# The gradient of the convolution kernel: its last quarters computed two steps apart, its stores and two groups of weight-gradient stores issued by ScalarE

## Chip, core and metric

The kernel runs on one core of one Trainium2 chip. The metric is the device time of one execution in microseconds (us). The times given for the kernel before are three runs: 480.13, 480.28 and 480.67 us, median 480.28 us.

## What is computed

The reference takes a normalised input, adds a gated convolution branch and a gated linear branch to it, and returns the output together with the gradients of all nine inputs for a given `grad_out`:

```python
x = A_q; xn = layernorm(x)
kv = causal_shift_conv(k, shift_k) * v              # 4 taps
y  = irfft(rfft(kv, 2S) * rfft(ssm_k, 2S))[:S] + kv * ssm_D
A  = xn * y
B  = ((xn @ w_gate) * (xn @ w_up)) @ w_down
out = x + A + B                                      # out_0
out_1 .. out_9 = vjp(grad_out)                       # q, k, v, shift_k, ssm_k, ssm_D, w_gate, w_up, w_down
```

S is 2048 tokens, D 512 channels, F 1376 hidden features, all arrays are bf16. Four outputs matter here: out_5, the gradient of ssm_k (512 x 2048, 2 MB); out_7 and out_8, the gradients of w_gate and w_up (512 x 1376 each); out_9, the gradient of w_down (1376 x 512).

## The kernel before, in words

The program is written in a tile framework: Python generators emit the instructions of all engines, and the framework puts each engine's instructions in an order, adds the semaphore waits and rotates the buffers. Loads and stores are issued by SyncE (SP, in program order), a few by ScalarE (ACT). All stores of the same engine stand in one queue: a store whose data isn't ready holds back those behind it.

The work comes in three phases. The first and second (up to some 330 us) run the gated linear branch chunk by chunk and, beside it, the transforms of the convolution. The third, `dw()` (L1048), is where the change lies. It goes over the hidden features in eleven blocks `FBLK` (ten of 128 columns, the last of 96), called fb 0 to 10. For each block TensorE computes

- `pd` (`down_grad`, L1022; matmuls in L1036, for the last block in L1029): the block of the gradient of w_down. ACT casts it to `od`, SP stores it to out_9 (L1043). The last block is done in two halves after everything else (L1024 to L1033); its first half is stored by SP, its second by ACT (L1032).
- `pu` (L1060 to L1067): the block of the gradients of w_gate and w_up, as four groups of 16 matmuls with 256 columns (192 for the last block). ACT casts it to `og` (L1073), which holds two blocks; after every second block, and after the last, `og` is stored to out_7 and out_8 (L1074 to L1077). So the stores come after fb 1, 3, 5, 7, 9 and 10. Before the change only those of fb 10 are issued by ACT.
- transposes of the hidden activations for the next block: `pt` (L859), and `pt7` (L829), whose cast `nat7` gives the last two of the 16 token rows.

`dw()` yields six times for each block. At each yield, numbered n, the loop at the end (L1201 to L1206) lets four side generators emit a piece of their own work. Each side is a list `[start, step, generator]`: when n has reached `start`, `step` is added to `start` and one piece is emitted.

```python
sides = [every(seq(inv_y(), load_dk()), 0, 3), every(dsk_gram(), 27, 2), every(inv_dk(), 35, 3), every(ew(), 10, 3)]
```

The third of them, `sides[2]`, is `inv_dk()` (L989): the gradient of ssm_k. It works in quarters `rq` of the 16 token rows, and in halves `b` of the four channel blocks. For each it emits 16 matmuls of 128 columns into a PSUM tile `po` (L1001) and a cast by ACT into `o5t` (L1003), a tile of 128 x 4 x 128 x 16 that is filled quarter by quarter. When a half b of the last quarter (rq 3) is cast, two channel blocks are whole, and each is stored as 512 KB in rows of 4 KB (L1008): four stores in all. In the kernel before, the pieces rq 2 b 1, rq 3 b 0 and rq 3 b 1 fall on n = 53, 56 and 59: after the `pu` of fb 8, ahead of the `pu` of fb 9, and behind it.

The fourth side, `ew()` (L1184), emits the elementwise end on VectorE (DVE): `final` (L1131) and `bwd` (L1108), whose results `o0`, `e` and `dk` are stored by SP (`put_late`, L1179, L1181) to out_0, out_1 and out_2.

PSUM tiles of the kinds `po`, `pu`, `pt7` take turns in three buffers, `pd` in two. DMAs take eight completion semaphores in turn, whichever engine issues them; the built program lets a DMA wait until the last DMA of its semaphore has landed.

Of the kernel before, what the change touches and what calls it, by code (L numbers as in the profile page):

```python
# [24 lines left out]
NFB = len(FBLK)  # L25
# [165 lines left out]
def kernel(  # L191
# [24 lines left out]
    nc = tc.nc  # L216
# [14 lines left out]
    def cs(c):  # L231
        return slice(c * 128, (c + 1) * 128)

    def act(o, i):
        nc.scalar.copy(o, i)  # L235
# [16 lines left out]
    def P2(name, shape, dt=F32):  # L252
        return ps2.tile(shape, dt, name=name, tag="p2")
# [374 lines left out]
    def seq(*its):  # L628
        for it in its:
            for _ in it:  # L630
                yield
# [156 lines left out]
    LG = {}  # L788

    def load_hb(fb):  # L790
        f0, fw = FBLK[fb]
        t = CP["b"].tile([P, NCH - 1, 3, 256], BF, name="hb")
        nc.sync.dma_start(t[:fw], HDD[:fw, fb])
        hbs[fb] = t
# [29 lines left out]
    def last_t(fb):  # L824
        f0, fw = FBLK[fb]
        pt = P2("pt7", [P, 3, 2, P], BF)
        for t in range(3):
            for h in range(2):
                nc.tensor.transpose(pt[:, t, h, :fw], hds[1][:fw, fb, t, h * 128:h * 128 + 128], ident[:fw, :fw])  # L829
        n7 = c2b.tile([P, 3, 2, P], BF, name="nat7", tag="dd")  # L830
        act(n7[:, :, :, :fw], pt[:, :, :, :fw])
        nats[fb, 1] = n7
# [7 lines left out]
    def nat_d(fb, r):  # L840
        f0, fw = FBLK[fb]
        if fb not in TURNED:
            return nats[fb, 1][:, :, r, :fw]
        return nats[fb, 0][r // 2][:, 1:3, r % 2, :] if r < R - 2 else nats[fb, 1][:, 1:3, r % 2, :fw]

    def hid_t(fb, t):
        if fb in TURNED:
            return
        f0, fw = FBLK[fb]
        hb = hbs.pop(fb) if t == 2 else hbs[fb]  # L850
        if t == 0:
            nats[fb, 0] = CP["n"].tile([P, R, P], BF, name="nath")
        elif t == 1:
            nats[fb, 1] = CP["n"].tile([P, 2, R, P], BF, name="natd", bufs=2)
        dst = nats[fb, 0] if t == 0 else nats[fb, 1][:, t - 1]
        pt = P2("pt", [P, R, P], BF)
        for r in range(R):
            hs = hb[:fw, r // 2, t] if r < R - 2 else hds[1][:fw, fb, t]
            nc.tensor.transpose(pt[:, r, :fw], hs[:, (r % 2) * 128:(r % 2) * 128 + 128], ident[:fw, :fw])  # L859
        act(dst[:, :, :fw], pt[:, :, :fw])  # L860
# [114 lines left out]
    def load_gk(rq):  # L975
        return load_g1(2, 4 * rq)
# [3 lines left out]
    def load_gk_last():  # L980
        ts = {}
        for h in range(2):
            for c in range(2):
                t = c2b.tile([P, 2, D], BF, name=("vb", "kb")[c])
                LG["gk"] = nc.sync.dma_start(t[:], GD[2, :, c, 12 + 2 * h:14 + 2 * h, :])
                ts[c, h] = t
        return lambda c, i: ts[c, i // 2][:, i % 2]

    def inv_dk():  # L989
        o5t = c2.tile([P, NC4, P, R], BF, name="o5t", tag="o5k")  # L990
        o5 = out_5.rearrange("(c q) s -> c q s", q=P)
        for rq in range(4):
            gk = gks.pop(0)
            if rq == 0:
                gk_last = load_gk_last()
            for b in range(2):
                po = P2("po", [P, 2, 4, P])
                for h in range(2):
                    for i in range(4):
                        for c in range(2):  # L1000
                            nc.tensor.matmul(po[:, h, i, :], lhsT=(gk_last(c, i) if rq == 3 else gk[:, c, i])[:, cs(2 * b + h)], rhs=TB.IW[:, c, :],  # L1001
                                             start=(c == 0), stop=(c == 1))
                act(o5t[:, 2 * b:2 * b + 2, :, 4 * rq:4 * rq + 4], po[:].rearrange("q h r s -> q h s r"))  # L1003
                if b == 1 and rq < 2:
                    gks.append(load_gk(2) if rq == 0 else None)
                if rq == 3:
                    for c in (2 * b, 2 * b + 1):
                        nc.sync.dma_start(o5[c], o5t[:, c].rearrange("q s r -> q (s r)"))  # L1008
                yield
            if rq == 0:  # L1010
                yield from put_dD(o5t)

    def put_dD(o5t):
        act(dDs[:], o5t[:, :, 0, 0])
        yield
        pt = P1("ptd", [P, P], BF)
        nc.tensor.transpose(pt[:NC4, :], dDs[:], ident[:])
        dDt = c2.tile([NC4, P], BF, name="dDt")
        act(dDt[:], pt[:NC4, :])
        nc.sync.dma_start(out_6.rearrange("(c p) -> c p", p=128), dDt[:])  # L1020

    def down_grad(fb):  # L1022
        f0, fw = FBLK[fb]
        if fb + 1 == NFB:  # L1024
            for h, q in ((0, nc.sync), (1, nc.scalar)):
                hc = slice(256 * h, 256 * h + 256)
                pd = P1("pd", [P, 256])
                for r in range(R):
                    nc.tensor.matmul(pd[:fw, :], lhsT=nat_h(fb, r), rhs=goC[:, r, hc], start=(r == 0), stop=(r == R - 1))  # L1029
                od = c2b.tile([P, D], BF, name="od")  # L1030
                act(od[:fw, :256], pd[:fw])
                q.dma_start(out_9[f0:f0 + fw, hc], od[:fw, :256])  # L1032
            return  # L1033
        pd = P1("pd", [P, D])
        for r in range(R):
            nc.tensor.matmul(pd[:fw, :], lhsT=nat_h(fb, r), rhs=goC[:, r, :], start=(r == 0), stop=(r == R - 1))  # L1036
            if r == R // 2 - 1 and fb:
                hid_t(fb, 2)
                if fb + 2 < NFB:
                    load_h(fb + 2)  # L1040
        od = c2b.tile([P, D], BF, name="od")
        act(od[:fw], pd[:fw])
        nc.sync.dma_start(out_9[f0:f0 + fw, :], od[:fw])  # L1043
# [4 lines left out]
    def dw():  # L1048
        og = None
        load_hb(2)  # L1050
        for fb, (f0, fw) in enumerate(FBLK):
            last = fb + 1 == NFB
            if not last:
                down_grad(fb)
                yield
                hid_t(fb + 1, 0)
                hid_t(fb + 1, 1)
                yield
                yield
            pu = P2("pu", [P, NC4, 2, P])  # L1060
            if fb % 2 == 0:
                og = c2b.tile([P, 2, NC4, P], BF, name="og1", tag="dd") if last else c2.tile([P, 2, NC4, 2 * P], BF, name="og")
            q0 = (fb % 2) * P
            for c in range(NC4):
                for r in range(R):
                    nc.tensor.matmul(pu[:, c, :, :fw], lhsT=xnC[:, r, cs(c)], rhs=nat_d(fb, r),  # L1066
                                     start=(r == 0), stop=(r == R - 1))  # L1067
                if c == 1:
                    yield
                    if fb + 1 in TURNED:  # L1070
                        last_t(fb + 1)
                    yield
            act(og[:, :, :, q0:q0 + fw].rearrange("p t c f -> p c t f"), pu[:, :, :, :fw])  # L1073
            if fb % 2 == 1 or last:  # L1074
                a = f0 - q0
                for t, o in enumerate((out_7, out_8)):
                    LG["og"] = (nc.scalar if last else nc.sync).dma_start(o[:, a:f0 + fw].rearrange("(c p) f -> p c f", p=128), og[:, t, :, :q0 + fw])  # L1077
            yield
            if last:
                down_grad(fb)  # L1080
                yield
# [87 lines left out]
    def every(gen, start, step):  # L1169
        return [start, step, gen]  # L1170
# [13 lines left out]
    def ew():  # L1184
        with tc.issue_after(DKS[2].ins):
            load_fin(0)
        yield
        for f in tail:
            put_late()
            f()  # L1190
            yield
        with tc.issue_after(LG["og"].ins):
            put_late()
        yield

    def load_dk():
        gks.append(load_gk(0))
        gks.append(load_gk(1))
        yield

    sides = [every(seq(inv_y(), load_dk()), 0, 3), every(dsk_gram(), 27, 2), every(inv_dk(), 35, 3), every(ew(), 10, 3)]  # L1201
    for n, _ in enumerate(dw()):
        for sd in sides:
            if n >= sd[0]:
                sd[0] += sd[1]
                next(sd[2], None)  # L1206
# [33 lines left out]
```

## Time and profile before

The profile is of one execution on this core. Its own time was 478.65 us and its span 476.9 us, so 1.75 us lie outside the span; the median of the three timed runs is 480.28 us.

| what | value |
|---|---|
| time of the profiled execution | 478.65 us |
| its span | 476.9 us |
| busy: TensorE (PE), weight loads, DVE, ACT | 98%, 65%, 71%, 64% of the span |
| granted TensorE clock | 0.999 |
| DMA | 139.86 MB, 293 GB/s over the span |
| SP's DMA queue (q1), ACT's (q10) | 137.65 MB, 1.56 MB |
| stores of `o5t` | 4 of 512 KB, 5.2 us from issue to landing (median) |
| stores of `og` | 10 of 256 KB by SP, 6.3 us; 2 of 96 KB by ACT, 4.4 us |

A row of the timeline gives the start, the length, the engine, the line of the code and the tiles (`out<-in`). A name ending in q (SPq, ACTq) is an engine's sequencer: for a DMA the length is that of its issue, and the transfer comes after. A row of the table by stage gives busy time of each engine in a stretch, the TensorE clock, the share of time in which the DMA engines were busy (it can come out a little over 1) and what they moved.

### The profile page before, as it was taken

What the parts mean: (1) busy time and instruction counts of PE and PEld (TensorE: products, weight loads), DVE (VectorE), ACT (ScalarE), POOL (GpSimd) and SP (SyncE); (2) the same over time, 40 slices, a digit from 0 to 9 for tenths busy, and PEclk for the clock granted to TensorE, in tenths of its full rate; (3) what the DMA queues carried; (4) which work ended last, traced back from release to release, by engine and by line L of the source; (5) the groups of instructions that cost most, each with busy time, mean ns of one, the idle gap of its engine ahead of it and who ended that gap; (6) DMA issues with size and microseconds to landing.
All of it is one profiled execution on the core that took longest, in us unless ns stands there. A gap on an engine that the chain in (4) does not pass through costs nothing.

```text
span 476.9 us, 10353 instructions
## 1 busy us (share of the span) xinstructions
PE 465.1 (98%) x4263; PEld 310.7 (65%) x4263; DVE 339.3 (71%) x609; ACT 304.6 (64%) x357; POOL 13.9 (3%) x30
## 2 busy tenths in 40 slices
PE   7999999999999999999999999999999999999995
PEld 6876755547648547447447743567776787777794
DVE  7889979989356567686857877122237899899692
ACT  4957767759577778779879976275675554333331
POOL 8000000000000000000000000110000000000000
PEclk9999999999999999999999999999999999999999
DMA  8999999899997958968977459999999999999948
GB/s 269 372 376 374 296 267 350 316 327 327 322 298 258 264 196 266 278 208 253 301 222 253 158 186 384 350 336 309 337 375 381 366 294 323 329 263 277 227 148 295
DMA packets 116917, 139.86 MB, mean 293 GB/s; under 512 B 44776, under 2 KB 90249, under 8 KB 115463
## 3 DMA queue, kind: packets, MB, share of 16 engines
q1 hardware_dynamic: 114230, 137.65, 91.7%
q10 hardware_dynamic: 2640, 1.56, 1.2%
q8 instruction: 33, 0.54, 0.5%
q14 instruction: 14, 0.11, 0.1%
HBM read 65.70 MB, written 63.41 MB: 271 GB/s over the span
## 4 chain that ended last, share of the span: by engine, by line
PE 82%; DMA 10%; DVE 6%; ACT 1%; issue 1%; DVEq 0%; ACTq 0%
PE pu L1066 16%; PE px L555 14%; PE pgu L512 13%; PE pd L1036 7%; PE py L548 7%; PE pdh L518 6%; PE pt L859 3%; PE pq L932 3%; PE ps L584 3%; DMA ssk<-in_A_ssm_k_dram 3%; PE pg L613 3%; PE pf L370 3%; DMA hb<-HDD 2%; DMA x_b<-in_A_q_dram 2%; PE pk L1089 2%; PE po L1001 2%
## 5 line engine op out<-in xcount | busy, mean ns | idle before, releaser
L555 PE MATMUL px<-WT,hd 128*128 128x512 bf16 (+1 forms) x352 | 81.0, 380 | 0.0
L1066 PEld LDWEIGHTS <-xnC 128*128 128x128 bf16 x704 | 67.1, 98 | 8.1 <-issue 0.4
L555 PEld LDWEIGHTS <-hd 128*128 128x128 bf16 (+1 forms) x352 | 32.8, 98 | 44.4 <-issue 7.7
L235 ACT CAST gu<-pgu 128x1024 bf16<-128x1024 f32 (+1 forms) x48 | 45.4, 945 | 16.7 <-PE pgu L512 16.2
L235 ACT CAST GO<-pg 128x1024 bf16<-128x1024 f32 x48 | 46.2, 1015 | 13.8 <-issue 7.2
L235 ACT CAST SP<-ps 128x1024 bf16<-128x1024 f32 x47 | 45.6, 1026 | 13.7 <-PE ps L584 11.8
L600 DVE TENSOR_TENSOR T<-SP 128x2048 bf16<-128x2048 bf16 x24 | 29.3, 1222 | 34.8 <-ACT SP L235 34.7
L512 PE MATMUL pgu<-xt,Wu 128*128 128x256 bf16 (+1 forms) x352 | 53.1, 273 | 0.7 <-DVE kn L238 0.6
L512 PE MATMUL pgu<-xt,Wg 128*128 128x256 bf16 (+1 forms) x352 | 52.8, 273 | 0.3 <-DMA Wg<-in_B_w_gate_dram 0.3
L518 PE MATMUL pdh<-gt,WdT 128*128 128x256 bf16 (+1 forms) x352 | 46.9, 273 | 0.1
L235 ACT CAST fst<-pf 128x1024 bf16<-128x1024 f32 x44 | 42.7, 1031 | 5.5 <-ACT fst L235 1.9
L1066 PE MATMUL pu<-natd,xnC 128*128 128x256 bf16 x384 | 43.9, 273 | 0.0
L512 PEld LDWEIGHTS <-Wu 128*128 128x128 bf16 (+1 forms) x352 | 33.0, 100 | 14.9 <-issue 9.8
L548 PE MATMUL py<-Wd,hd 128*128 128x512 bf16 (+1 forms) x176 | 41.4, 380 | 0.0
L518 PEld LDWEIGHTS <-WdT 128*128 128x128 bf16 (+1 forms) x352 | 34.9, 100 | 4.8 <-issue 0.2
L512 PEld LDWEIGHTS <-Wg 128*128 128x128 bf16 (+1 forms) x352 | 34.8, 100 | 4.2 <-DMA Wg<-in_B_w_gate_dram 0.6
L1066 PE MATMUL pu<-natT,xnC 128*128 128x256 bf16 (+1 forms) x280 | 32.3, 267 | 0.0
L533 DVE TENSOR_TENSOR hd<-gu,dh 128x1024 bf16<-128x1024 bf16 (+1 forms) x48 | 30.8, 642 | 0.8
L532 DVE TENSOR_TENSOR hd<-gu 128x512 bf16<-128x512 bf16 (+1 forms) x48 | 19.1, 397 | 17.0 <-ACT gu L235 17.0
L235 ACT CAST og<-pu 128x1024 bf16<-128x1024 f32 (+1 forms) x11 | 10.9, 993 | 30.4 <-PE pu L1066 24.5
L548 PEld LDWEIGHTS <-hd 128*128 128x128 bf16 (+1 forms) x176 | 16.5, 98 | 20.8 <-issue 3.1
L600 DVE TENSOR_TENSOR U<-SP 128x2048 bf16<-128x2048 bf16 x24 | 29.2, 1218 | 0.0
(178 smaller groups left out, 686.3 us busy)
## 6 DMA issues: line engine op xcount, KB each, us to landing
HDD<-hd SPq DMA_DIRECT2D x35, 384.0 KB, 4.6
FD<-fst SPq DMA_DIRECT2D x24, 512.0 KB, 5.0
X<-FD SPq DMA_DIRECT2D x24, 512.0 KB, 5.5
GD<-GO SPq DMA_DIRECT2D x24, 512.0 KB, 3.8
g<-GD SPq DMA_DIRECT2D x11, 1024.0 KB, 8.7
hb<-HDD SPq DMA_DIRECT2D x6, 1344.0 KB, 9.9
bb<-BX SPq DMA_DIRECT2D x8, 512.0 KB, 6.5
BX<-bx SPq DMA_DIRECT2D x7, 512.0 KB, 4.0
```

The costliest lines, as they stand in the source:

```text
L235: nc.scalar.copy(o, i)
L370: nc.tensor.matmul(pf[:, c, :], lhsT=TB.W1[:, c, :], rhs=src[:, i, :], start=True, stop=not point)
L512: nc.tensor.matmul(pgu[:w, i, t, :], lhsT=W[:, c, f0:f0 + w], rhs=xt[:, :, c, :], start=(c == 0), stop=(c == NC4 - 1))
L518: nc.tensor.matmul(pdh[:w, i, :], lhsT=WdT[:, c, f0:f0 + w], rhs=gt[:, :, c, :], start=(c == 0), stop=(c == NC4 - 1))
L532: nc.vector.tensor_tensor(hd[:fw, fb0:fb0 + n, 0, :], gu[:fw, :n, 0, :], gu[:fw, :n, 1, :], op=ALU.mult)
L533: nc.vector.tensor_tensor(hd[:fw, fb0:fb0 + n, 1:3, :], gu[:fw, :n], dh[:fw, :n].unsqueeze(2).to_broadcast((fw, n, 2, 256)), op=ALU.mult)
L548: nc.tensor.matmul(py[:], lhsT=hd[:fw, fb, 0, ss], rhs=Wd[:fw, fb, :], start=(fb == 0), stop=(fb == NFB - 1))
L555: nc.tensor.matmul(px[:], lhsT=hd[:fw, fb, t, ss], rhs=W[:fw, fb, :], start=(t == 1 and fb == 0), stop=(t == 2 and fb == NFB - 1))
L584: nc.tensor.matmul(ps[32 * q:32 * q + 32, a, :], lhsT=TB.EF[64 * a:64 * a + 64, 4 * g + q, ri].rearrange("p k j -> p (k j)"), rhs=X[64 * a ...
L600: tt(W[:].rearrange("p c a d -> p c (a d)"), A[:, i:i + 1].rearrange("p c a d -> p c (a d)").to_broadcast((P, 2, 2 * D)), B[:].rearrange(" ...
L1036: nc.tensor.matmul(pd[:fw, :], lhsT=nat_h(fb, r), rhs=goC[:, r, :], start=(r == 0), stop=(r == R - 1))
L1066: nc.tensor.matmul(pu[:, c, :, :fw], lhsT=xnC[:, r, cs(c)], rhs=nat_d(fb, r), start=(r == 0), stop=(r == R - 1))
```

## The change

Two things are changed, and no arithmetic.

```diff
         for rq in range(4):
             gk = gks.pop(0)
+            if rq == 2:
+                sides[2][1] = 2
             if rq == 0:
                 gk_last = load_gk_last()
...
                 if rq == 3:
                     for c in (2 * b, 2 * b + 1):
-                        nc.sync.dma_start(o5[c], o5t[:, c].rearrange("q s r -> q (s r)"))
+                        nc.scalar.dma_start(o5[c], o5t[:, c].rearrange("q s r -> q (s r)"))
...
                 for t, o in enumerate((out_7, out_8)):
-                    LG["og"] = (nc.scalar if last else nc.sync).dma_start(o[:, a:f0 + fw].rearrange("(c p) f -> p c f", p=128), og[:, t, :, :q0 + fw])
+                    LG["og"] = (nc.scalar if fb + 2 >= NFB else nc.sync).dma_start(o[:, a:f0 + fw].rearrange("(c p) f -> p c f", p=128), og[:, t, :, :q0 + fw])
```

From the piece rq 2 b 0 on, the side `inv_dk()` advances by two steps instead of three. The step of three that was already added at that piece still holds once, so rq 2 b 1 stays on n = 53, rq 3 b 0 comes at 55 instead of 56, and rq 3 b 1 at 57 instead of 59: in the middle of the `pu` of fb 9, after two of its four groups. The four stores of `o5t`, and the two stores of `og` after fb 9, are issued by ACT instead of SP.

## The prediction

> **What bounds the kernel now.** I read the chain of waits first, then its end in order of time, then a table of the last 24 us by stage, then what SP waited for, and last the timeline around its issues. By the chain TensorE (PE) carries the kernel:
>
> ```profile
> PE 82%; DMA 10%; DVE 6%; ACT 1%; issue 1%; DVEq 0%; ACTq 0%
> ```
>
> The end of that chain, start and length in us:
>
> ```profile
> 461.32 0.89 PE po L1001 x16
> 462.21 5.28 PE pu L1066 x64
> 467.49 3.51 PE pd L1029 x32
> 471.00 0.02 issue
> 471.02 0.37 ACT od L235
> ```
>
> PE runs without a gap to 471.0, and the last cast ends at 471.39. The span ends at 476.9. So 5.5 us at the end belong neither to PE nor to ACT. The table by stage says whose they are (busy us of PE, PEld, DVE, ACT, POOL, the clock, the DMA share, GB/s):
>
> ```profile
> 456.00:459.00 3.00, 3.00 (x34) 2.71 (x32) 2.93 (x7) 0.64 (x1) 0.00 (x0) 1.00 0.51 196
> 459.00:462.00 3.00, 3.00 (x38) 2.78 (x36) 2.86 (x4) 0.65 (x1) 0.00 (x0) 1.00 0.23 87
> 462.00:465.00 3.00, 3.00 (x40) 3.00 (x38) 2.90 (x4) 1.28 (x2) 0.00 (x0) 1.00 0.09 31
> 465.00:468.00 3.00, 3.00 (x38) 3.00 (x36) 2.86 (x5) 0.42 (x1) 0.00 (x0) 1.00 1.03 387
> 468.00:471.00 3.00, 2.98 (x28) 2.73 (x25) 0.63 (x1) 0.75 (x2) 0.00 (x0) 1.00 1.05 303
> 474.00:475.00 1.00, 0.00 (x0) 0.00 (x0) 0.00 (x0) 0.00 (x0) 0.00 (x0) 1.00 1.00 328
> 475.00:476.00 1.00, 0.00 (x0) 0.00 (x0) 0.00 (x0) 0.00 (x0) 0.00 (x0) 0.79 0.41 106
> 476.00:476.90 0.90, 0.00 (x0) 0.00 (x0) 0.00 (x0) 0.00 (x0) 0.00 (x0) 0.50 0.00 0
> ```
>
> From 465 to 475.4 the DMA engines are full; from 459 to 465 they stand almost idle. About 0.85 us after the last transfer the span ends. Why the idle time comes before the jam is in SP's waits and issues:
>
> ```profile
> SPq L1181 <- DVE dk L1120: 4.2, 1, 4.2
> SPq L1235 <- DMA out_dram<-o5t: 2.4, 1, 2.4
> ```
> ```profile
> 463.96 0.33 SPq L1181 DMA_DIRECT2D out_dram<-dk  x1
> 464.39 0.38 SPq L1043 DMA_DIRECT2D out_dram<-od  x1
> 464.86 0.89 SPq L1008 DMA_DIRECT2D out_dram<-o5t  x2
> 465.85 2.17 SPq L1077 DMA_DIRECT2D out_dram<-og  x2
> 468.12 1.75 SPq L1008 DMA_DIRECT2D out_dram<-o5t  x2
> 469.95 1.33 SPq L1181 DMA_DIRECT2D out_dram<-dk  x1
> 471.38 1.07 SPq L1032 DMA_DIRECT2D out_dram<-od  x1
> 471.42 0.35 ACTq L1032 DMA_DIRECT2D out_dram<-od  x1
> ```
>
> The first half of `o5t` is cast at 454.11 + 1.01 = 455.1, but its two stores stand in SP's queue behind a `dk` that DVE finishes at 463.9, and so start at 464.86, almost 10 us late. From then on SP and ACT issue 2048 (o5t) + 512 + 192 (og) + 256 (dk) + 96 (od) KB, with the dk and od just before 3488 KB or 3.57 MB; the table moves 3.5 MB from 465 to 476. **The end is a drain of late stores**, at some 340 GB/s.
>
> **The change, part by part.** The built programs are the same, instruction for instruction and wait for wait, up to about 455 us on every engine; only the last 22 us can differ, and DVE's list not at all.
>
> *The moved po.* 16 matmuls, 0.89 us, go from 461.32 to 457.57 (after two groups of the `pu` of fb 9). PE does the same work, so its sum is 0 as long as nothing new is waited for. The last `pu` follows at 462.2 as before; it waits, in the built program, for the cast of the moved po (458.5 + 1.02 = 459.5) and at its 15th matmul (463.4) for `nat7` (0.64, now 460.2). Both covers are about 3 us. `pt7` waits for a cast that ended at 455.1. The og cast, which po used to lie beside, isn't waited for by PE.
>
> *ACT's six issues.* No row shows a 512 KB store issued by ACT under these conditions; its issue lies between 0.35 (ACT, od) and 1.57 (SP, og in a full queue, the longest of its four); I take 0.4 to 0.9, o5t's own four (0.40 to 0.87). Each issue also waits for the last DMA on its semaphore, and ACT's casts queue behind it:
> - o5t 1 and 2 wait for the od of 452.42 (landed 456.1 by the trace's semaphore records) and the e of 453.51 (457.3). ACT is free at about 457.8 to 458.2. Behind stands the cast of the moved po, ready at 458.5: nothing lost.
> - o5t 3 and 4 wait for stores that landed by 457.9 and 458.5. They go out at 460.2 to 461.2, after nat7; the next cast, og, is ready at 462.2.
> - og 1 goes at 463.3. **og 2 waits for the dk that SP issues at 463.96**, which lands 2.1 us later, at 466.0. ACT stands blocked for 2 us, then issues until 466.5 to 467.4 (0.41 to 1.29). Behind it stands the cast of the last og, ready at 467.5: nothing lost. After that, cast 0.80, two issues 1.42 and the first od cast 0.37 must be done by 471.02: og 2 may end as late as 468.3, so dk may land 1.0 us later than before, at least.
>
> *SP.* The last dk, ready at 467.94 + 0.69 = 468.63, goes at once instead of at 469.95. SP's last od shares a semaphore with it, so it waits until this dk has landed: 2.1 us by the two dk and e that SP issued into idle engines (459.32, 463.96), 5.7 by the one of 469.95 in the jam. The og stores of fb 10 (192 KB in rows of 192 bytes, ACT, 468.4 to 469.8) lie beside it; I take 2.7, landing at 471.4.
>
> *The drain.* 2 MB leave the tail: 1 MB flows at about 457.5 to 461, 1 MB at 461 to 464.5, both in the idle stretch. From 463.3 on remain 3488 - 2048 = 1440 KB, 4.3 us of engine time within 8 us. The jam is gone.
>
> *The sum.* PE's end 471.0 stays, ACT's od goes at 471.42 as before. A lone od store (464.39, idle engines) landed 2.0 us after its issue began: 473.4; plus 0.85 is 474.3. SP's od goes at 471.4 and meets ACT's issue; with 2.0 to 3.3 (0.35 to 1.07 of issue, and leftovers of og) it lands at 473.4 to 474.7, span 474.3 to 475.5. I take 474.7: **2.2 us less** than 476.9. On the profiled execution's own time that is 478.65 - 2.2 = 476.4; the timed median is 1.63 higher, 480.28, and the same subtraction gives **478.1 us**. The most that can be had is 2.6, since PE's end and the last od stay: 477.7.
>
> *A rule against it.* The row is the 0.09 share from 462 to 465 while two finished 512 KB stores were waiting. The Trainium skill, "DMA: Bandwidth & Descriptors", section "Issuing engines are not separate DMA queues", says that DMAs of all issuing engines run on the same 16 engines, so that issuing from several saves only the sequencer's time for the issue. By that rule alone nothing of the drain would go, and the kernel would stay at 480.3; this is rival 1. The trace speaks against reading it so here, since what is saved is a wait in SP's order, not bandwidth.
>
> **The rivals.**
> 1. *The drain stays* (the stores start no earlier, because ACT is held at the semaphore waits, or the engines deliver no more): the end is again the last landing near 476, 480.0 to 480.3 us. For it: six new waits on ACT. Against: all landings named above are in the trace, and idle engines follow. Chance 0.07.
> 2. *A new chain ends it*: DVE's last dk at 468.63, its landing, then SP's od. If dk lands 3.4 to 4.1 us after its issue (the o of 455.09 took 3.4, behind a few others; 4.1 is near the middle of 2.1 and 5.7), the od goes at 472.1 to 472.8 and with 2.0 to 3.3 lands at 474.1 to 476.1; the middle gives a span of 476.0, gain 0.9, 479.4. For it: the shared semaphore is certain. Against: little else is in flight. Chance 0.12, half of it on either side of a gain of 0.96.
> 3. *Slower: ACT blocked at og 2.* If the dk of 463.96 lands later than about 467.1, each further us moves the last og cast, its stores and both od stores by one; from a landing at 469.7 on (2.6 us more) the kernel is slower than before, and at 471 it ends at 478.2, 481.6 us. For it: o5t 3 and 4 and og 1 now run just before this dk. Against: they are 1.25 MB, 3.9 us from 461 on, done about 465. Chance 0.06.
>
> **How the numbers follow.** Forecast (gain 1.3 to 2.7): 0.75; rival 1: 0.07, rival 2: 0.12, rival 3: 0.06. A measurement of this kernel tells 0.2%, 0.96 us, from no change. Faster by more: 0.75 and half of rival 2, 0.81. Within: the other half and rival 1, 0.13. Slower by more: rival 3, 0.06. The range runs from the largest gain with the scatter of the runs (2.6 + 0.4: 477.3) to just past rival 2's middle (479.6), which leaves out rivals 1 and 3 and the worse part of rival 2, 0.18.
>
> **What would show it.** Right: o5t's stores issued by ACT at about 456, 457, 460 and 461, DMA share above 0.5 from 459 to 465, below 0.7 from 471 on; PE's last matmul at 471.0; the last cast at 471.0 to 471.4; SP's end wait no longer on o5t but on od. Wrong: a gap in PE before 471, an og cast of fb 10 that starts after 468.3 (rival 3), an SP od issued after 472.5 (rival 2), or stores of o5t landing after 466 (rival 1).

## The result, and the profile after

The changed kernel took 476.35 us (median of six runs, 475.25 to 477.91), beside 481.01 us for the kernel before in its six: ratio 0.9897, 95% interval 0.9869 to 0.9926. The forecast was 478.1 us in a range of 477.3 to 479.6; the kernel is faster by twice as much as I said, and the time lies below the range. Eighteen more runs of the same kernel in the experiments below had medians of 477.45 and 477.76 us, so the first six were on the low side. Over all, the mean of 24 runs after is 477.3 us and that of 90 runs of before, 26 of them beside other kernels only, 480.7 us: 3.4 us, 0.70%. The two repeats alone give less: 477.64 us against 480.63 us for the runs of before beside them, 3.0 us, with a 95% interval of about 2.4 to 3.6 estimated from the scatter of the runs. So a good part of the first 4.7 us was luck.

The profiled execution took 475.32 us, its span is 473.5 us (before: 478.65 and 476.9). The page gives the chain that ended last, by engine:

```profile
PE 85%; DMA 8%; DVE 5%; ACT 1%; issue 1%; ACTq 0%
```

The end of that chain in order of time (start and length in us):

```profile
456.90 0.89 PE po L1003 x16
457.80 0.26 PE pt L829 x6
458.05 8.78 PE pu L1068 x96
466.83 3.51 PE pd L1031 x32
470.34 0.02 issue
470.36 0.37 ACT od L235
```

The moved po sits between the groups of the tenth `pu`, and from there PE runs without a gap to 470.34. The same end was at 471.0 before; the 0.66 us between them arise at 44 and at 307 us, long before the first instruction that the change touches, and are scatter between executions. From PE's end to the end of the span it was 5.9 us, and is 3.2. The table by stage (busy us of the engines, the clock, the DMA share, GB/s):

```profile
456.00:459.00 3.00, 3.00 (x42) 2.80 (x40) 2.93 (x9) 1.16 (x2) 0.00 (x0) 1.00 1.06 414
459.00:462.00 3.00, 3.00 (x32) 2.74 (x30) 2.86 (x4) 0.81 (x2) 0.00 (x0) 1.00 1.02 414
462.00:465.00 3.00, 3.00 (x39) 3.00 (x37) 2.90 (x4) 0.60 (x1) 0.00 (x0) 1.00 0.63 249
468.00:471.00 3.00, 2.32 (x22) 2.07 (x19) 0.95 (x2) 0.74 (x2) 0.00 (x0) 1.00 0.73 183
471.00:472.00 1.00, 0.00 (x0) 0.00 (x0) 0.00 (x0) 0.00 (x0) 0.00 (x0) 1.00 0.25 57
472.00:473.00 1.00, 0.00 (x0) 0.00 (x0) 0.00 (x0) 0.00 (x0) 0.00 (x0) 1.00 0.17 41
```

The idle stretch from 459 to 465 is in use (share 1.02 and 0.63, where it was 0.23 and 0.09), and behind 471 the DMA engines have little left to do. The timeline's issues, and what SP waited for at the end:

```profile
456.21 1.59 ACTq L1010 DMA_DIRECT2D out_dram<-o5t  x2
458.75 0.65 ACT L235 COPY nat<-pt 128x576 bf16<-128x576 bf16 x1
458.88 0.86 ACTq L1010 DMA_DIRECT2D out_dram<-o5t  x2
464.88 1.94 ACTq L1079 DMA_DIRECT2D out_dram<-og  x2
469.01 0.33 SPq L1183 DMA_DIRECT2D out_dram<-dk  x1
470.76 0.35 ACTq L1034 DMA_DIRECT2D out_dram<-od  x1
471.08 0.33 SPq L1034 DMA_DIRECT2D out_dram<-od  x1
```
```profile
SPq L1034 <- DMA out_dram<-dk: 1.7, 1, 1.7
```

All four o5t stores are issued by 459.7. SP's last od doesn't wait for the drain any more but for the landing of the last dk, as the prediction said of the shared semaphore.

### The profile page after: what moved, and what is told of

It is laid out like the page before. It is cut to its first block, busy times and chain, and to the rows that moved or that the text cites. A ratio compares the mean times of both kernels' runs of the same rounds, so it can differ in the third digit from the quotient of the medians.

```text
span 473.5 us, 10352 instructions
## 1 busy us (share of the span) xinstructions
PE 464.8 (98%) x4263; PEld 310.5 (66%) x4263; DVE 339.4 (72%) x609; ACT 304.6 (64%) x357; POOL 13.9 (3%) x30
## 4 chain that ended last, share of the span: by engine, by line
PE 85%; DMA 8%; DVE 5%; ACT 1%; issue 1%; ACTq 0%
PE pu L1068 16%; PE px L555 16%; PE pgu L512 13%; PE py L548 8%; PE pd L1038 7%; PE pdh L518 6%; PE pt L859 3%; PE pq L932 3%; PE ps L584 3%; PE pg L613 3%; DMA ssk<-in_A_ssm_k_dram 3%; PE pf L370 3%; DMA x_b<-in_A_q_dram 2%; PE pk L1091 2%; PE po L1003 2%; DMA XN<-x_b 1%
```

## The experiments

So the picture of the drain was right and the size wrong. Two questions: where do the 3.4 to 4.7 us come from, when the tails of the two first profiles differ by 2.7 only; and which part of the change earns them.

A word on names in the expectations. In the first four, D, E and T are theories. From the fifth on, D is a time: the start of the `dk` store of bwd 6 (463.96 in the first profile), which is the last thing that holds SP's queue ahead of the o5t stores. The tail is the time from the start of ACT's last cast to the end of the span. Theory P, in the later ones, is that the end hangs on PE's end.

All ratios are to the kernel before in rounds on the same chip:

| run | what it is | ratio, 95% interval | D | D to end | tail |
|---|---|---|---|---|---|
| first profile | before | | 463.96 | 12.9 | 5.8 |
| ctl1 | before | 0.999, 0.997 to 1.001 | 464.73 | 12.8 | 7.1 |
| ctl2 | before | 1.000, 0.998 to 1.002 | 467.32 | 12.9 | 7.2 |
| step1 | step alone | 0.999, 0.997 to 1.001 | 465.53 | 12.9 | 7.6 |
| ogact | og on ACT alone | 0.996, 0.994 to 0.999 | 464.55 | 11.3 | 5.4 |
| lightb | before, less DVE work | 0.995, 0.993 to 0.998 | 463.37 | 14.1 | 5.7 |
| heavyb | before, more DVE work | 1.005, 1.003 to 1.007 | 470.58 | 12.5 | 8.4 |
| first profile | the change | 0.990, 0.987 to 0.993 | 464.31 | 9.2 | 3.2 |
| aft1 | the change | 0.993, 0.990 to 0.996 | 466.75 | 9.1 | 3.6 |
| aft2 | the change | 0.994, 0.992 to 0.996 | 466.22 | 9.3 | 3.9 |
| actboth1 | stores on ACT, no step | 0.992, 0.990 to 0.994 | 466.92 | 9.8 | 4.0 |
| step_o5 | step, o5t on ACT, og on SP | 0.993, 0.990 to 0.996 | 467.63 | 8.4 | 2.9 |
| lighta | the change, less DVE work | 0.992, 0.989 to 0.995 | 463.56 | 11.1 | 3.0 |
| heavya | the change, more DVE work | 0.998, 0.996 to 1.000 | 468.06 | 9.3 | 5.9 |

### The two kernels again (ctl1, aft1)

No edit. Expected of ctl1:

> The kernel before, unchanged, as a control. Theory D (the change only empties the drain of stores behind the last matmul; what the two first profiles differ in before 455 us is scatter between executions): ratio 1.000, last matmul ends anywhere from 470 to 474 us, and from there to the end of the span 5.9 us as in the first profile. Theory E (the change also shortens something in front of the last matmul, worth the 2 us by which the measured 4.7 us exceed the 2.7 us seen in the tails): the same tail, 5.9 us. Theory T (the tail of before is longer in most executions than in the one first profiled): tail 7 us or more.

Expected of aft1:

> The changed kernel again, on the chip of the control. Theory D: ratio 0.994 (2.7 us less), tail 3.2 us, last matmul scattering over the same 470 to 474 us as the control's. Theory E: ratio 0.990 again, tail 3.2 us. Theory T: ratio 0.990, tail 3.2 us, with the control's tail 7 us or more.

The kernel before has a tail of 7.1 us here, not 5.8; aft1 has 3.6 us. Theory T is the one that holds: the execution profiled first had an unusually short tail. The control's lines of SP say why. Here are SP's `dk` and its last `od`, the span is 477.6 us:

```profile
464.73 0.33 SPq L1181 DMA_DIRECT2D out_dram<-dk  x1
472.87 1.19 SPq L1032 DMA_DIRECT2D out_dram<-od  x1
```

PE's end is 0.57 us earlier than in the first profile (last cast at 470.45, was 471.02), but the dk is 0.77 us later, and the span ends 12.84 us behind it, where it was 12.91. The end keeps its distance from DVE's dk, not from PE. What makes DVE late against PE are two of its waits in front of the change; among its groups from 392 to 415 us (busy, mean ns, then the idle time ahead and what ended it), first in the first profile of before, then in ctl1:

```profile
L1140 DVE TENSOR_TENSOR o<-o,bb 128x1024 bf16<-128x1024 bf16 x2 | 1.4, 692 | 1.1 <-DMA bb<-BX 1.1
L1139 DVE TENSOR_TENSOR o<-xnC,yC 128x1024 bf16<-128x1024 bf16 x2 | 1.4, 688 | 1.5 <-DMA out_dram<-o 1.5
```
```profile
L1139 DVE TENSOR_TENSOR o<-xnC,yC 128x1024 bf16<-128x1024 bf16 x2 | 1.4, 688 | 3.1 <-DMA out_dram<-o 3.1
L1140 DVE TENSOR_TENSOR o<-o,bb 128x1024 bf16<-128x1024 bf16 x2 | 1.4, 687 | 1.8 <-DMA bb<-BX 1.8
```

DVE waits there for a load and for a store that frees a buffer: 2.6 us in the first profile, 4.9 in ctl1, and 4.9 in aft1 as well. Of these 2.3 us, 1.2 are made up by two other waits that are longer in the first profile (0.5 for an `e` at 411 us, 3.7 instead of 3.0 for an `o` later); of the rest 0.8 us is left at D. The first profile's DVE was early.

The granted clock of the timed runs says that this was the exception. In all fourteen profiles it is still 1.00 at PE's last matmul, so matmuls at a lower clock are no cause of the differences here; it falls to 0.50 between 2.0 and 5.3 us behind that, in the idle tail. So the mean clock of an execution falls as its tail grows. It was 0.999 in the first profile of before; of the 84 runs of before beside the experiments only two had 0.999 or more, and the mean was 0.996, while 22 of the 24 runs of the change had 0.999 or more.

In aft1 (span 475.9) SP's last two stores are:

```profile
471.45 0.33 SPq L1183 DMA_DIRECT2D out_dram<-dk  x1
473.52 0.33 SPq L1034 DMA_DIRECT2D out_dram<-od  x1
```

The od goes when the dk has landed, 2.07 us later, and 4.4 us behind the dk the span ends. That gave theory S: **before ends at D + 12.9; the changed kernel at D + 9.2 (dk 4.7 behind D, then 4.5) or at PE's last cast + 3.2, whichever is later.** The gain is then 3.7 us as a rule, and less only where DVE is as early as in the first profile. (The 3.2 comes from the first profile of the change, where SP's od still waited for the dk. Where it waited for no dk, in lighta and step_o5 below, the end is at the last cast + 3.0 and + 2.9.)

### The change in two halves (step1, actboth1)

Step alone:

```diff
+            if rq == 2:
+                sides[2][1] = 2
```

> Only the step of two: the last po is computed between the groups of the tenth pu, all stores stay on SP. Theory D: no gain, ratio 0.999 to 1.001, tail 5.5 to 5.9 us, since all four o5t stores still stand behind the dk that DVE finishes at 464 and drain from there. Rival (the earlier po is the cause): 2 us or more less, tail near 3.2 us.

Ratio 0.999, tail 7.6 us, D + 12.9: no gain. The four o5t stores stand behind D together, instead of in pairs around og, and drain as before.

The stores alone:

```diff
-                        nc.sync.dma_start(o5[c], ...
+                        nc.scalar.dma_start(o5[c], ...
-                    LG["og"] = (nc.scalar if last else nc.sync)...
+                    LG["og"] = (nc.scalar if fb + 2 >= NFB else nc.sync)...
```

> Only the stores on ScalarE, with the step of three. Theory D: the first two o5t stores go at 456 and 457, the last two at 464.3 and 466.4 (the fourth waits for the landing of the dk of 464); 2.5 MB remain from 462.4 on, 7.2 us at 340 GB/s, done by about 470.5, so nearly the whole gain: ratio 0.994 to 0.996, tail 3.2 to 4.2 us. Rival (the step is needed for the gain): half of it, 1.3 us, tail 4.5 us or more.

Ratio 0.992 (0.990 to 0.994), as good as the whole change. The fourth o5t store goes only at 470.1, as it waits for the landing of D's dk and holds up a cast of ACT for it, and D to end is 9.8 instead of 9.2; in the time this isn't seen. So the gain comes from the queue in which the stores stand, and the step adds nothing that these runs can tell.

### Less and more DVE work (lightb, lighta, heavyb, heavya)

If S holds, DVE's work ahead of D moves the end of both kernels, and PE's end does so of the changed one alone. Less (the kernels leave out two of the four taps in bwd of b = 6, so a part of the gradient of k is wrong in them):

```diff
-        for j in (0, 2):
+        for j in ((0,) if b == 6 else (0, 2)):
```

> The kernel before, with less DVE work ahead of the dk that holds SP's queue: bwd of b = 6 leaves out taps 2 and 3 (three DVE instructions, some 2.6 us), so these rows of the gradient of k are not whole. D is the start of that dk's store (463.96, 464.73 in the two profiles of before). Theory S (SP's queue follows DVE, and before ends at D + 12.9 whatever PE does): D comes about 2.5 us earlier against PE's end, the span still ends at D + 12.9, tail 4.5 to 5.1 us, ratio 0.9945 to 0.996. Theory P (the end hangs on PE's end, and tails differ by chance in the drain): ratio 0.999 to 1.001.

> The changed kernel with the same taps left out. Theory S: after ends at the later of PE's last cast + 3.2 and D + 9.15 (last dk 4.7 behind D, its landing, then SP's od); with D 2.5 us earlier the first holds always: tail 3.2 us, SP's od no longer waiting for a dk, 0 to 0.6 us better than the changed kernel, ratio 0.990 to 0.993. So the gain against the kernel with the same taps left out is only 1.5 us where it was 3.7. Theory P: the gain against it stays what it was.

Before with less DVE work has the ratio 0.995 (2.4 us less than before): theory P, no effect, lies outside its interval. Its profile didn't end at D + 12.9 but at D + 14.1. One row accounts for it, the od behind the dk:

```profile
463.79 1.61 SPq L1043 DMA_DIRECT2D out_dram<-od  x1
```

That issue took 0.38 us in the control, 1.23 us less, and everything behind it is later by as much. The trace has one 16 KB packet of the instruction queue (q8 in the page) starting at 463.6 and lasting 1.4 us; that it is the cause of the long issue was not tested. With less DVE work the changed kernel is at 0.992 with a tail of 3.0 us, and SP's od no longer waits for a dk: the last cast bounds it. That cast comes 0.4 us behind PE's end, since the dk at D took 5.5 us to land beside the o5t stores and og 2, which waits for it, was issued only at 469.07. The two medians lie 2.3 us apart (478.43 and 476.13), where those of before and after were 3.4 in the rounds with ctl1 and 2.9 in those with ctl2; the intervals are too wide to show that this gain is smaller, so this part of S isn't shown.

More:

```diff
-            nc.vector.tensor_tensor(t[:], src, w, op=ALU.mult)
+            for _ in range(3 if b == 6 and j == 2 else 1):
+                nc.vector.tensor_tensor(t[:], src, w, op=ALU.mult)
```

> The kernel before with more DVE work: in bwd of b = 6 one multiplication is done three times, some 2.2 to 2.4 us more ahead of D (the start of the dk store that holds SP's queue); in SP's list one od store comes to stand ahead of this dk instead of behind it. Theory S (before ends at D + 12.9): D comes 2.2 us later against PE's end, the end 1.8 to 2.4 us later, ratio 1.004 to 1.005, tail 8.5 to 10 us, PE's end untouched. Theory P (the end hangs on PE's end): ratio 0.999 to 1.001.

> The changed kernel with the same extra DVE work. Theory S (after ends at the later of the last cast + 3.2 and D + 9.15): the second holds always, SP's last od waits for the last dk, tail 5 to 6 us, 1.6 to 2.4 us slower than the changed kernel, ratio against before 0.996 to 0.998. If PE's end alone bounds the changed kernel: no difference to it, ratio 0.9925, tail 3.2 us.

The ends are as S had them. heavyb: 1.0048 (1.0028 to 1.0069), and its span of 483.1 us ends 12.5 us behind this row, 0.4 less than 12.9 since one od, 0.38 us of issue, now stands ahead of it:

```profile
470.58 0.33 SPq L1182 DMA_DIRECT2D out_dram<-dk  x1
```

heavya: 479.38 us, 1.6 us more than the changed kernel beside it (aft2, 477.76), end at D + 9.3, tail 5.9. So DVE bounds the changed kernel too as soon as it is late; PE's end alone would have left it at 0.9925. Who waits is not what was expected. The two dk and SP's last od:

```profile
468.06 5.03 SPq L1184 DMA_DIRECT2D out_dram<-dk  x2
473.19 0.38 SPq L1034 DMA_DIRECT2D out_dram<-od  x1
```

SP's od goes right behind the second dk, without waiting for its landing. With one od more ahead of D the semaphores fall differently in the built program, and it is ACT's last od that waits for the late dk: it was issued only at 474.87, 2.1 us behind the dk of 472.76.

### Which stores (ogact, step_o5)

```diff
-                    LG["og"] = (nc.scalar if last else nc.sync)...
+                    LG["og"] = (nc.scalar if fb + 2 >= NFB else nc.sync)...
```

> Only the og stores on ScalarE; o5t stays on SP behind D. Theory S: 512 KB, 1.5 us of engine time, start at 463 instead of standing between the o5t stores; the 2 MB of o5t still start at D + 0.9: span ends at D + 11.4 to D + 12.4, ratio 0.997 to 0.999, tail 5.5 to 7 us. Rival (the og stores carry the gain): tail below 4.5 us.

0.996 (0.994 to 0.999), D + 11.3: og alone is worth about half, a little more than expected. With the step and o5t on ACT, and og left on SP:

> The change without the og stores: these stay on SP. In the built program SP's last od then waits for an o5t store that has long landed instead of the last dk. Theory S: the end is PE's last cast + 3.2 always, D no longer matters: tail 3.1 to 3.3 us, ratio 0.990 to 0.993, some 0.3 us better than the change. Rival (og on ScalarE is part of the gain): the 512 KB of og behind D + 0.9 on SP lengthen the drain, tail 4 us or more.

0.9925 (0.9895 to 0.9955), tail 2.9 us, D + 8.4. SP's od went at 472.8 without waiting for a dk. So og needn't move once o5t has; the tail is the shortest of all that compute everything, but in time it can't be told from the change.

### Third profiles (ctl2, aft2)

> Before, a third profile. Theory S: the end lies 12.9 us behind D (to 14 where a fetch of instructions holds one DMA engine, as in the run with less DVE work), the tail is 6.5 to 8 us, not the 5.8 of the first profile. Theory P: tail 5.8 us.

> The changed kernel, a third profile and five more rounds. Theory S: tail 3.1 to 3.8 us, end at D + 9.1 to 9.2 where SP's last od waits for the last dk; ratio 0.991 to 0.993, as the difference of D + 12.9 and D + 9.15, 3.75 us, gives. Theory D, as in the prediction: ratio 0.9945 to 0.9955.

ctl2 ends at D + 12.9 with a tail of 7.2 us, and aft2 at D + 9.3 with 3.9. aft2's ratio is 0.994 (0.992 to 0.996); it lies between the two forecasts, outside both, and its interval reaches both. The distances from D are those of S: 12.84 to 12.91 us before and 9.14 to 9.33 after, in three profiles of each. Whether the times gain the 3.7 us that follow from them is not shown: the two repeats give 3.0 us (about 2.4 to 3.6), and only with the first set 3.4 (about 2.8 to 3.9). In aft2 the dk at D took 2.9 us to land, og 2 went at 469.1 and ACT's last cast came 0.3 us after PE's end: rival 3 in a small dose.

## Why the prediction was wrong

- *"The end is a drain of late stores"*: right, and so is what starts it, SP's queue behind DVE's dk. The share of the DMA engines (above 0.5 from 459 to 465, below 0.7 from 471 on), the issue times of o5t 1 and 2 (456.21 and 457.46; forecast about 456 and 457) and SP's od waiting for the dk came as written.
- **The step that failed is *The sum*, and with it "the most that can be had is 2.6, since PE's end and the last od stay".** It took the tail of before, 5.9 us from PE's end, as a property of the kernel. It is the difference of two ends that scatter against each other: the kernel ends at D + 12.9 (12.84 to 12.91 in four profiles with SP's list unchanged up to the o5t stores), and D lay 7.1 us ahead of the last cast in the first profile but 5.2 to 5.7 in ctl1, ctl2 and step1. I had written that the o5t stores stand behind a dk that DVE finishes, and yet hung the end on PE, whose share of the chain is 82%. Worked from D, the prediction's own rows give 12.9 against 4.7 (the last dk) + 2.1 (its landing) + 2.0 + 0.85 (the od and the end), 9.6: 3.3 us, wherever PE isn't later. Measured were 9.1 to 9.3, and so 3.5 to 3.8. The tails measured since are 6.7 us on the mean of three profiles of before and 3.6 of three after, 3.1 us, where the sum had 2.2.
- One term of the sum was also too large: from the issue of the last od to the end of the span it took 2.85 us at the least (2.0 + 0.85, from a 128 KB od). The 48 KB od that end the kernel took 2.4 us from SP (aft1, aft2) and 2.5 to 2.6 from ACT (step_o5, lighta). So the tail from the last cast can fall to 2.9 us, and "the most that can be had" is some 0.3 us more even in the first profile.
- The sign was there: the profiled execution was 1.63 us faster than the timed median, and I carried this over as a constant. It was an execution with a short tail, as the clock of the other runs shows; DVE's two waits at 395 and 410 us, 2.6 us in all, could have been asked what they depend on.
- The range was too narrow for another reason: I added 0.4 us for scatter, and took 480.28, the median of three runs, for the time of before. Single runs of before went from 477.5 to 483.9 us and medians of six runs after from 476.35 to 477.45. By the mean of the repeats, 477.6 us, the time lies inside the range, so that it lay below it in the first set is partly luck; the gain of 3.0 to 3.4 us is still above the 2.6 that I held possible, though the interval of the two repeats alone (2.4 to 3.6) reaches below it.
- *SP*, rival 2: the wait of SP's last od for the last dk came in the first profile, aft1, aft2 and actboth1, and sets the end of the last three. Its size was too high: in the first profile and aft1 the od went 2.07 us after the dk's issue, in aft2 2.26, where I took 2.7.
- *ACT's issues*: og 1 went at 464.88, not 463.3. It waited for the e that SP had issued at 459.67 and that landed 5.1 us later; I had taken 2.1 us for stores of this size, from a row in a stretch that the change fills. It cost nothing, since og 2 waited for the dk at 466.4 anyway.
- *The moved po*: 0, as said, and step1 shows that it also gains nothing.
- *Rival 1 and the rule*: the stores start 8.6 us earlier and the drain goes, which refutes rival 1. The Trainium skill, "DMA: Bandwidth & Descriptors", "Issuing engines are not separate DMA queues", is right that the transfers interleave on the same engines: the e took 5.1 us beside the o5t stores, 2.1 without. But "will only save the time on the sequencer" doesn't cover this case: actboth1 changes the issuing engine and nothing else and gains 3.8 us by its medians (477.04 and 480.84), 3.3 by its means. The measurement decides: what is saved is the wait behind the dk in SP's queue.

## What to carry to other kernels

Find the event from which the end keeps a fixed distance, and count from there; an engine with 98% busy time and most of the chain need not be it. A tail read from one execution can be the difference of two scattering ends, so take it from several, or work out which end moves. In an in-order queue of stores, a store whose data comes late holds those that are ready: give them another queue, but look at which semaphores the new issues wait for.

## What the runs showed of the hardware

- ACT issues a DMA while it still runs a cast: the copy of 458.75 takes 0.65 us, the issue of o5t 3 began at 458.88. I had put the issue behind the copy.
- From 456 to 462 us of the changed kernel the DMA engines moved 414 GB/s, ACT's 512 KB stores in rows of 4 KB and SP's 256 KB stores beside them, more than the 340 I took from the jam.
- An issue by SP behind the o5t stores in its own queue took 1.07 to 1.34 us (the last dk 1.28, the last od 1.19 in ctl1). With those stores in ACT's queue the same two took 0.33 each, in all three profiles of the changed kernel. Long issues come elsewhere too (the od of 1.61 us in lightb).
- The granted TensorE clock stayed at 1.00 for 2.0 to 5.3 us after the last matmul and then fell to 0.50, in each of the fourteen profiles. A mean clock below 1 was here a sign of a long idle tail, not of slower matmuls.
